# A fused attention and mixer kernel: from a scheduler's order to an order fixed by hand

## The chip, the cores and the metric

The kernel runs on one core of one Trainium2 chip. A core has five engines, each with its own instruction queue: TensorE (PE, matrix products; its weight loads are listed as PEld), VectorE (DVE), ScalarE (ACT), GpSimd (POOL) and SyncE (SP, which here only issues transfers). Each engine executes its queue in order and waits at an instruction whose inputs or buffers are not ready. [...]

The metric is the device time of the program in microseconds (us), as the median of several runs. Lower is better.

## The reference

For a batch of 8 with 8 heads, 576 positions and 64 values per head, the reference computes a windowed attention and then one token-and-channel mixer block:

```
rel = pos[:, None] - pos[None, :]
mask_plain = (rel >= 0) & (rel < 32)                       # heads 0..3
mask_dil   = (rel >= 0) & (rel < 128) & (rel % 4 == 0)     # heads 4..7
attn = softmax(where(mask, q @ k.T / 8, -1e9))
x    = (attn @ v), heads joined to 512 channels            # (8, 576, 512)
h    = relu(x.T @ w_tok1) @ w_tok2                         # over positions, 576 -> 256 -> 576
u    = x + h.T
out  = u + relu(u @ w_ch1) @ w_ch2                         # over channels, 512 -> 1536 -> 512
```

Inputs and output are float32; the kernel works in float16 with float32 sums in PSUM.

## The kernel before, in words

The work of one batch has two parts.

The *fill* computes attention and the token mixing. For each of four pairs of heads (hp 0 and 1 plain, 2 and 3 dilated) it transposes q and k on PE (`transposes`, L241; PSUM tiles `tp_q`, `tp_k`) and copies the results to SBUF: k by DVE into `kt`, the first head of q by DVE and the second by ACT into `qz`. The scores of a pair (`scores_plain` L268, `scores_dil` L302; PSUM tiles `sc` and, for the ends of the sequence, `sm`) are exponentiated by ACT into `attp` or `attd`, and multiplied by 0/1 masks (`band`, `dtail`), by DVE for batch 0 and by POOL for all others; the small tail part of a pair has an exponential and a mask of its own. For the dilated pairs, q is kept in four residue classes of positions, r, each 144 wide, so the queries after position 512 are read from it with a stride. The values of a head (`values` L328, PSUM tile `av`) are nine or six small matmuls, a reciprocal and a product on DVE into `xn`. Then follow the token mixing's first layer (`emit_h1` L361, PSUM `h1p`, relu on ACT into `h1`), its second with the residual (`emit_u` L373, PSUM `up`, five adds on DVE into `u16` and `u16t`), and the transpose of u (`emit_uT` L395, PSUM `tpu`, four copies on DVE and ACT in turn into `uT`).

The *main* part computes the channel mixing (`gen_main`, L469): 24 groups of four matmuls of 128 x 288 (`gp`, L480) with a relu by ACT or DVE in turn into `gt`, and eight groups of 12 matmuls of 128 x 256 (`yp`, L491 and L496), with an add on DVE (`o32`, L499) and two output transfers on SP after each second one. Odd batches have one more group of 12 x 512 columns for the last 64 rows of two batches (L506).

PSUM is shared out by tags: three banks `main` (gp, yp), three `sc`, two `fl` (tp, av, h1p, up, tpu).

While the main part of batch b runs, the fill of batch b+1 runs too, and q, k and v of batch b+2 are loaded by SP (`emit_loads`) and cast to float16 (`gen_casts`: q and the tails on ACT, k and v on POOL). The kernel writes these as streams of steps with assumed costs, and `drive` (L516) takes the stream that is least far along:

```
best = min(live, key=lambda st: st[1] / st[2] + st[3])
```

The framework's scheduler then reorders the instructions on each engine by its own estimate. So the final order on an engine is not the order of the source.

Before the loop stands the head: batch 0's loads on SP (one at a time, tails first), the weights w1, w2, w3 and w4 on POOL's queue, the fill of batch 0 without a main part beside it, and the loads and casts of batch 1. The weights are held back by small copies (`gate`, L544) that write one element of the target once some other data has come.

Of the kernel before, what the change touches and what calls it, by code (L numbers as in the profile page):

```python
# [9 lines left out]
FP16 = mybir.dt.float16  # L10
# [4 lines left out]
B = 8  # L15
# [53 lines left out]
def kernel(  # L69
# [39 lines left out]
    ident = fixed("ident", [128, 128])  # L109
    perm = [fixed(f"perm{i}", [128, 128]) for i in range(2)]  # L110
    band = fixed("band", [128, 1, 1, BLK])
    dtail = fixed("dtail", [128, 1, 2, 64])
    nc.sync.dma_start(out=ident, in_=nc.inline_tensor(np.eye(128, dtype=np.float16), name="ident128").ap())
    for i in range(2):
        nc.sync.dma_start(out=perm[i], in_=nc.inline_tensor(_np_perm(i), name=f"perm{i}").ap())
# [11 lines left out]
    w2 = [fixed(f"w2_{i}", [128, 640]) for i in range(2)]  # L127
    w2p = [fixed(f"w2p_{i}", [128, 4, 128]) for i in range(2)]
    w3 = [fixed(f"w3_{i}", [128, DCH]) for i in range(4)]
    w4 = [fixed(f"w4_{i}", [128, DM]) for i in range(NMB)]  # L130

    def emit_fixed():
        for hp in range(4):
            nc.gpsimd.memset(qz[hp][64:128, 0], 0.0)
            nc.gpsimd.memset(qz[hp][0:64, 1], 0.0)
            nc.gpsimd.memset(kt[hp][:, S:640], 0.0)
        for i in range(2):
            a = attp[i]
            nc.gpsimd.memset(
                a[:, :, 0:PTL].rearrange("p h (b c) -> p h b c", c=PST)[:, :, :, BLK:PST], 0.0)  # L140
            nc.gpsimd.memset(a[:, :, PTL:PW], 1.0)
            nc.gpsimd.memset(attd[i][:, :, DTL:DW], 1.0)
        for i in range(2):
            nc.gpsimd.memset(vv[i][64:128, 4], 0.0)
            nc.gpsimd.memset(vv[i][:, :, :, 64:65], 1.0)
            nc.gpsimd.memset(vt[i][:, :, 64:65], 1.0)
            nc.gpsimd.memset(w2[i][:, S:640], 0.0)
            nc.gpsimd.memset(w1t[i], 0.0)

# [3 lines left out]
    def load_qk(b, nm):  # L153
        t = sb.tile([128, H, 4, D], FP32, tag=f"l_{nm}", bufs=1, name=f"l_{nm}_{b}")
        l32[(b, nm)] = t
        for hp in range(4):
            nc.sync.dma_start(
                out=t[:, 2 * hp:2 * hp + 2].rearrange("m h r d -> m h (r d)"),
                in_=SRC[nm][b, 2 * hp:2 * hp + 2, 0:512, :].rearrange("h (m r) d -> m h (r d)", r=4))

    def load_tails_qk(b):
        t = sb.tile([128, H, D], FP32, tag="lt", bufs=1, name=f"lt_{b}")
        l32[(b, "t")] = t
        nc.sync.dma_start(out=t[0:64], in_=q[b, :, 512:S, :].rearrange("h s d -> s h d"))
        nc.sync.dma_start(out=t[64:128], in_=k[b, :, 512:S, :].rearrange("h s d -> s h d"))
# [18 lines left out]
    def emit_loads(b):  # L184
        load_tails_qk(b)
        load_qk(b, "q")
        load_qk(b, "k")
        load_v(b)
# [27 lines left out]
    def gen_casts(b):  # L216
        cast_tails_qk(b, nc.scalar)
        yield 1
        for hp in range(4):
            cast_qk(b, "q", hp, nc.scalar)  # L220
            yield 1
            cast_qk(b, "k", hp, nc.gpsimd)
            yield 1
        for i in range(2):
            cast_vn(b, 2 * i, nc.gpsimd)
            yield 1
            cast_vn(b, 2 * i + 1, nc.gpsimd)
            yield 1
            cast_vd(b, 2 * i, nc.gpsimd)
            yield 1  # L230
        cast_tail_v(b, nc.gpsimd)
        cast_vx(b, nc.gpsimd)
        yield 1
# [7 lines left out]
    def transposes(b, nm, hp):  # L241
        c = c16[(b, nm)]
        p = bank("fl", 2, f"tp_{nm}_{b}_{hp}", FP16)
        grid = p[:, 0:4 * RS].rearrange("p (r i) -> p r i", i=RS)
        for r in range(4):
            nc.tensor.transpose(  # L246
                out=grid[:, r, 0:128],
                in_=c[:, r, 2 * hp:2 * hp + 2, :].rearrange("m h d -> m (h d)"), identity=ident)
        nc.tensor.transpose(  # L249
            out=grid[:, :, 128:RS],  # L250
            in_=c16[(b, "t")][:, 2 * hp:2 * hp + 2, :].rearrange("m h d -> m (h d)"),
            identity=perm[nm == "k"])
        got = grid[:, :, 0:MR].rearrange("p r m -> p m r")
        if nm == "k":
            copy(nc.vector, natural(kt[hp][:, 0:S]), got)
        else:
            for h, eng in ((0, nc.vector), (1, nc.scalar)):
                rows = slice(64 * h, 64 * h + 64)
                o = qz[hp][rows, h]
                if hp < 2:  # L260
                    copy(eng, natural(o), got[rows])
                else:
                    copy(eng, o.rearrange("p (r m) -> p r m", r=4), grid[rows, :, 0:MR])
# [4 lines left out]
    def scores_plain(b, hp):  # L268
# [30 lines left out]
        mult(eng, tl, tl, band[:, 0, :, 0:64])  # L299
        yield 0.21  # L300

    def scores_dil(b, hp):  # L302
# [3 lines left out]
        for h in range(2):  # L306
            p = bank("sc", 3, f"sc_{b}_{hp}_{h}")
            for r in range(4):
                nc.tensor.matmul(  # L309
                    out=p[:, 128 * r:128 * r + 128], lhsT=kt[hp][:, r:512:4],  # L310
                    rhs=qz[hp][:, h, MR * r:MR * r + 128], start=True, stop=True)
# [3 lines left out]
        for h in range(2):  # L315
            qt = qz[hp][:, h].rearrange("p (r m) -> p m r", r=4)[:, 128:MR]
            for x, keys in enumerate((kt[hp][:, 384:512], kt[hp][:, 512:640])):
                nc.tensor.matmul(out=p[:, 128 * h + 64 * x:128 * h + 64 * x + 64], lhsT=keys,
                                 rhs=qt, start=True, stop=True)
# [5 lines left out]
        mult(eng, tl, tl, dtail)  # L325
# [35 lines left out]
    def emit_h1(b, jb):  # L361
        x = xn[b]
        j = slice(128 * jb, 128 * jb + 128)
        p = bank("fl", 2, f"h1p_{b}_{jb}")
        for c, w in ((slice(0, 256), w1n), (slice(256, 512), w1p)):
            nc.tensor.matmul(out=p[:, c], lhsT=w1t[b % 2][:, j], rhs=x[:, 4, c], start=True, stop=False)
            for s in range(4):
                nc.tensor.matmul(out=p[:, c], lhsT=w[:, s, j], rhs=x[:, s, c], start=False, stop=(s == 3))  # L368
        t = sb.tile([128, DM], FP16, tag="h1", bufs=4, name=f"h1_{b}_{jb}")
        relu(nc.scalar, t, p)  # L370
        return t
# [23 lines left out]
    def emit_uT(b, cb):  # L395
# [5 lines left out]
        eng = nc.scalar if cb % 2 else nc.vector  # L401
# [16 lines left out]
    GAP = 1.2  # L418

    def gen_fill(b):  # L420
        xn[b] = sb.tile([128, 5, DM], FP16, tag="xn", bufs=2, name=f"xn_{b}")
        if b % 2 == 0:
            u16t[b // 2] = sb.tile([128, DM], FP16, tag="u16t", bufs=2, name=f"u16t_{b // 2}")
            nc.vector.memset(u16t[b // 2][64:128], 0.0)

        def tp(hp):
            for nm in ("q", "k"):
                transposes(b, nm, hp)
                yield 0.25

        def sc(hp):
            yield from (scores_plain if hp < 2 else scores_dil)(b, hp)

        def va(hp):
            for h in (2 * hp, 2 * hp + 1):
                values(b, h)
                yield 0.29 if hp < 2 else 0.18

        yield from tp(0)
        yield from tp(1)  # L440
        yield from sc(0)
        yield from tp(2)
        yield from sc(1)
        yield from va(0)
        yield from tp(3)
        yield from sc(2)
        yield from va(1)
        yield from sc(3)
        yield GAP
        yield from va(2)  # L450
        yield GAP
        yield from va(3)
        yield GAP
        h1 = []
        for jb in range(2):
            h1.append(emit_h1(b, jb))
            yield 1.1
        yield GAP
        for s in (4, 0, 1, 2, 3):
            emit_u(b, s, h1)  # L460
            yield 0.44
        yield GAP
        for cb in range(4):
            emit_uT(b, cb)
            yield 0.25

    FILL = 2.0 + 1.22 + 1.13 + 1.88 + 2.2 + 2.2 + 1.0 + 5 * GAP

    def gen_main(b):  # L469
# [16 lines left out]
        for s in range(5 if odd else 4):  # L486
            p = bank("main", 3, f"yp_{b}_{s}")
            o32 = sb.tile([128, DM], FP32, tag="o32", bufs=3, name=f"o32_{b}_{s}")
            if s < 4:
                for mb in range(NMB):  # L490
                    nc.tensor.matmul(  # L491
                        out=p[:, 0:256], lhsT=gt[(b // 2, mb)][:, m0 + 128 * s:m0 + 128 * s + 128],
                        rhs=w4[mb][:, 0:256], start=(mb == 0), stop=(mb == NMB - 1))
                yield 1.31
                for mb in range(NMB):
                    nc.tensor.matmul(  # L496
                        out=p[:, 256:512], lhsT=gt[(b // 2, mb)][:, m0 + s:m0 + 512:4],
                        rhs=w4[mb][:, 256:512], start=(mb == 0), stop=(mb == NMB - 1))
                nc.vector.tensor_tensor(out=o32, in0=p, in1=u16[(b, s)], op=ALU.add)  # L499
                nc.sync.dma_start(out=out[b, 128 * s:128 * s + 128, 0:256], in_=o32[:, 0:256])  # L500
                nc.sync.dma_start(
                    out=out[b, 0:512, 256:512].rearrange("(m r) c -> r m c", r=4)[s], in_=o32[:, 256:512])
                yield 1.31
            else:
                for mb in range(NMB):
                    nc.tensor.matmul(out=p, lhsT=gt[(b // 2, mb)][:, 512:640], rhs=w4[mb],  # L506
                                     start=(mb == 0), stop=(mb == NMB - 1))
                nc.vector.tensor_tensor(out=o32, in0=p, in1=u16t[b // 2], op=ALU.add)
                nc.sync.dma_start(out=out[b - 1, 512:S, :], in_=o32[0:64])
                nc.sync.dma_start(out=out[b, 512:S, :], in_=o32[64:128])  # L510
                yield 2.6

    def main_cost(b):
# [105 lines left out]
```

## Time and profile before

| | us |
|---|---|
| median of 3 runs | 361.34 (360.73 to 362.38) |
| the profiled execution | 363.2 |
| its span, first to last instruction | 361.4 |
| PE busy | 309.3 (86%) |
| DVE busy | 186.3 (52%) |
| ACT busy | 146.2 (40%) |
| POOL busy | 146.3 (40%) |
| mean granted PE clock | 0.969 |
| DMA, all queues | 43.52 MB, mean 120 GB/s |

The page counts an engine as busy while an instruction of it executes. PE's matmuls overlap each other: the duration of one (288 ns for `gp`) is more than its share of the time (four in 0.49 us). A list of waits names the waiting engine, the line and the operation it stood at, and after the arrow the engine and line that released it, with the total in us, the number of waits and the longest. A timeline row gives the start, the length, the engine, the line, the operation and its tiles. A group row gives busy time and mean duration, and after the bar the idle time just before it with its releaser. The lines are those of the kernel before.

### The profile page before, as it was taken

What the parts mean: (1) busy time and instruction counts of PE and PEld (TensorE: products, weight loads), DVE (VectorE), ACT (ScalarE), POOL (GpSimd) and SP (SyncE); (2) the same over time, 40 slices, a digit from 0 to 9 for tenths busy, and PEclk for the clock granted to TensorE, in tenths of its full rate; (3) what the DMA queues carried; (4) which work ended last, traced back from release to release, by engine and by line L of the source; (5) the groups of instructions that cost most, each with busy time, mean ns of one, the idle gap of its engine ahead of it and who ended that gap; (6) DMA issues with size and microseconds to landing.
All of it is one profiled execution on the core that took longest, in us unless ns stands there. A gap on an engine that the chain in (4) does not pass through costs nothing.

```text
span 361.4 us, 7958 instructions
## 1 busy us (share of the span) xinstructions
PE 309.3 (86%) x3200; PEld 261.9 (72%) x3200; DVE 186.3 (52%) x401; ACT 146.2 (40%) x316; POOL 146.3 (40%) x201
## 2 busy tenths in 40 slices
PE   0626897499989997899899997899899998999994
PEld 0625576288877976688787976689788976888792
DVE  1727465226654456536664556536664456645421
ACT  2644277220683027721683027721682037412400
POOL 8774166932197006920296006920292006600000
PEclk9965899989999999999999999999999999999998
DMA  5999989856619520592019420532000120002012
GB/s 155 258 218 250 240 207 306 250 129 189 162 44 279 146 76 15 149 261 85 33 62 260 150 83 6 158 106 89 32 0 2 65 83 0 3 31 86 3 60 87
DMA packets 69588, 43.52 MB, mean 120 GB/s; under 512 B 37296, under 2 KB 68400, under 8 KB 69552
## 3 DMA queue, kind: packets, MB, share of 16 engines
q1 hardware_dynamic: 66128, 38.98, 38.2%
q0 software_dynamic: 3424, 4.03, 6.5%
q8 instruction: 25, 0.41, 0.5%
q14 instruction: 11, 0.09, 0.1%
HBM read 37.59 MB, written 9.44 MB: 130 GB/s over the span
## 4 chain that ended last, share of the span: by engine, by line
PE 53%; POOL 6%; ACT 5%; DVE 2%; issue 1%; DMA 1%; ACTq 0%; POOLq 0%
PE gp L480 13%; PE yp L496 10%; PE yp L491 10%; POOL attp L106 4%; PE h1p L368 3%; PE yp L506 3%; POOL attd L106 2%; ACT qz L94 2%; PE up L377 2%; PE up L380 1%; PE sc L309 1%; PE tp_q L246 1%; DVE qz L96 1%; PE tpu L413 1%; ACT attp L279 1%
## 5 line engine op out<-in xcount | busy, mean ns | idle before, releaser
L480 PE MATMUL gp<-uT,w 128*128 128x288 f16 x768 | 114.5, 288 | 1.9 <-ACT gt L100 1.9
L106 POOL TENSOR_TENSOR attp<-attp,band 128x1280 f16<-128x1280 f16 (+1 forms) x28 | 41.6, 1516 | 127.1 <-ACT attp L292 127.0
L480 PEld LDWEIGHTS <-w 128*128 128x128 f16 x768 | 71.1, 99 | 17.3 <-issue 2.6
L100 ACT ACTIVATE gt<-gp 128x288 f16<-128x288 f32 x96 | 39.7, 421 | 57.9 <-PE gp L480 57.6
L102 DVE TENSOR_SCALAR gt<-gp 128x288 f16<-128x288 f32 x96 | 43.2, 453 | 35.6 <-PE gp L480 32.1
L499 DVE TENSOR_TENSOR o<-yp,u 128x512 f32<-128x512 f32 x32 | 22.1, 692 | 56.2 <-PE yp L496 53.2
L491 PE MATMUL yp<-w,gt 128*128 128x256 f16 x384 | 48.5, 273 | 0.0
L496 PE MATMUL yp<-w,gt 128*128 128x256 f16 x384 | 47.2, 273 | 0.0
L496 PEld LDWEIGHTS <-gt 128*128 128x128 f16 x384 | 41.9, 114 | 0.3
L94 ACT COPY uT<-tpu 128x576 f16<-128x576 f16 x16 | 10.2, 639 | 74.6 <-PE tpu L407 69.8
L491 PEld LDWEIGHTS <-gt 128*128 128x128 f16 x384 | 37.3, 98 | 4.3
L106 DVE TENSOR_TENSOR xn<-av,rec 128x320 f16<-128x320 f32 x64 | 30.3, 487 | 1.3
L106 POOL TENSOR_TENSOR attd<-attd,band 128x1024 f16<-128x1024 f16 x14 | 29.8, 2129 | 1.7 <-ACT attd L312 1.6
L339 PE MATMUL av<-vv,attp 128*128 128x65 f16 x128 | 12.5, 200 | 18.8 <-POOL attp L106 12.1
L358 DVE RECIPROCAL rec<-av 128x5 f32<-128x5 f32 x64 | 11.2, 185 | 31.4 <-PE av L345 20.4
L246 PE MATMUL tp_q<-ident,c_q 128*128 128x128 f16 x128 | 13.4, 229 | 13.3 <-ACT c_q L94 9.3
L96 DVE COPY kt<-tp_k 128x576 f16<-128x576 f16 x32 | 23.9, 746 | 1.7 <-PE tp_k L249 1.6
L94 ACT COPY qz<-tp_q 64x576 f16<-64x576 f16 x32 | 20.3, 634 | 8.8 <-DVE qz L96 8.2
L383 DVE TENSOR_TENSOR u<-up,xn 128x512 f16<-128x512 f32 x32 | 21.2, 685 | 2.9 <-PE up L380 2.2
L246 PEld LDWEIGHTS <-c_q 128*128 128x128 f16 x128 | 9.9, 101 | 17.5 <-ACT c_q L94 10.9
L94 ACT CAST c_q<-l_q 128x512 f16<-128x512 f32 x32 | 19.6, 632 | 7.3 <-DMA l_q<-in_q_dram 3.6
L312 ACT ACTIVATE attd<-sc 128x512 f16<-128x512 f32 x32 | 18.7, 607 | 8.7 <-PE sc L309 8.5
(99 smaller groups left out, 515.2 us busy)
## 6 DMA issues: line engine op xcount, KB each, us to landing
out_dram<-o SPq DMA_DIRECT2D x72, 128.0 KB, 2.0
l_q<-in_q_dram SPq DMA_DIRECT2D x32, 256.0 KB, 4.5
l_k<-in_k_dram SPq DMA_DIRECT2D x32, 256.0 KB, 5.5
l_vn<-in_v_dram SPq DMA_DIRECT2D x32, 128.0 KB, 5.4
l_vd<-in_v_dram SPq DMA_DIRECT2D x16, 256.0 KB, 4.3
w<-in_moe_w_ch_dram POOLq DMA_DIRECT2D x12, 128.0 KB, 8.1
w<-in_moe_w_ch_dram POOLq DMA_DIRECT2D x4, 384.0 KB, 11.1
lt<-in_q_dram SPq DMA_DIRECT2D x8, 128.0 KB, 3.3
```

Source lines behind the costliest of these rows:

```text
L94: nc.scalar.copy(out=out, in_=in_)
L96: eng.tensor_copy(out=out, in_=in_)
L100: nc.scalar.activation(out=out, in_=in_, func=AF.Relu)
L102: eng.tensor_scalar_max(out=out, in0=in_, scalar1=0.0)
L106: eng.tensor_tensor(out=out, in0=x, in1=y, op=ALU.mult)
L246: nc.tensor.transpose(out=grid[:, r, 0:128], in_=c[:, r, 2 * hp:2 * hp + 2, :].rearrange("m h d -> m (h d)"), identity=ident)
L312: nc.scalar.activation(out=a[:, h, 0:DTL], in_=p, func=AF.Exp, scale=0.125)
L383: nc.vector.tensor_tensor(out=t, in0=p, in1=xn[b][:, s], op=ALU.add)
L480: nc.tensor.matmul(out=p[:, 0:288], lhsT=w3[cb][:, 128 * mb:128 * mb + 128], rhs=uT[(b, cb)][:, 288 * sh:288 * sh + 288], start=(cb == 0), ...
L491: nc.tensor.matmul(out=p[:, 0:256], lhsT=gt[(b // 2, mb)][:, m0 + 128 * s:m0 + 128 * s + 128], rhs=w4[mb][:, 0:256], start=(mb == 0), stop ...
L496: nc.tensor.matmul(out=p[:, 256:512], lhsT=gt[(b // 2, mb)][:, m0 + s:m0 + 512:4], rhs=w4[mb][:, 256:512], start=(mb == 0), stop=(mb == NM ...
L499: nc.vector.tensor_tensor(out=o32, in0=p, in1=u16[(b, s)], op=ALU.add)
```

## The change

`drive`, `gen_fill` and `gen_casts` go. The kernel calls `tc.manual_schedule()`, so each engine executes in source order, and the source fixes that order:

```diff
+    def fill_steps(b):
...
+        for hp, at in ((0, 0.2), (1, 1.6), (2, 4.6), (3, 8.0)):
+            for i, nm in enumerate(("q", "k")):
+                steps.append((at + 0.7 * i, 0.28, lambda nm=nm, hp=hp: transposes(b, nm, hp)))
+        for hp, at in ((0, 3.0), (1, 6.4), (2, 9.8), (3, 12.6)):
+            scores(hp, at)
+        for hp, at in ((0, 12.0), (1, 14.6), (2, 18.4), (3, 21.4)):
+            for h in range(2):
+                steps.append((at + 0.7 * h, 0.29 if hp < 2 else 0.18,
+                              lambda h=h, hp=hp: values(b, 2 * hp + h)))
+        for half, at in ((0, 19.4), (1, 24.0)):
+            for jb in range(2):
+                steps.append((at + 0.7 * jb, 0.55, lambda jb=jb, half=half: emit_h1(b, jb, half, h1[jb])))
+        for i, s in enumerate((4, 0, 1, 2, 3)):
+            steps.append((26.4 + 0.9 * i, 0.44, lambda s=s: emit_u(b, s, h1)))
         for cb in range(4):
+            steps.append((31.4 + 0.6 * cb, 0.28, lambda cb=cb: emit_uT(b, cb)))
+        return steps
...
+    def interleave(main, steps):
+        steps = sorted(steps, key=lambda st: st[0])
+        t = 0.0
+        while main is not None or steps:
+            if steps and (main is None or steps[0][0] <= t):
+                _, cost, fn = steps.pop(0)
+                fn()
+                t += cost
+            else:
+                try:
+                    t += next(main)
+                except StopIteration:
+                    main = None
...
     for b in range(B):
+        steps = []
+        if b + 2 < B:
+            emit_loads_qk(b + 2)
+            load_v(b + 2)
+            steps += [(19.0 + 0.9 * i, 0.0, f) for i, f in enumerate(cast_steps(b + 2))]
         if b + 1 < B:
+            steps += fill_steps(b + 1)
+        interleave(gen_main(b), steps)
```

`t` is an emission clock in assumed us; it decides only the order.

Work also changes engine. All casts of a later batch run on POOL (`cast_steps`: tails, q and k in turn, v, 17 in all). `kt` is copied by ACT, and so are the second halves of `uT` (cb 2 and 3; cb 0 and 1 on DVE). The tail masks go to DVE for every batch, and the memsets of `qz` and `kt` too. For hp 2 and 3, q is transposed flat, with its classes 128 wide and the positions from 512 on in one run of 64, so that the tail scores read it without a stride:

```diff
+        flat = nm == "q" and hp >= 2
         for r in range(4):
             nc.tensor.transpose(
+                out=p[:, 128 * r:128 * r + 128] if flat else grid[:, r, 0:128],
...
+        if flat:
+            nc.tensor.transpose(out=p[:, 512:640], in_=tail, identity=ident)
+            nc.vector.tensor_copy(out=qz[hp][0:64, 0], in_=p[0:64, 0:S])
+            nc.scalar.copy(out=qz[hp][64:128, 1], in_=p[64:128, 0:S])
+            return
...
         if nm == "k":
-            copy(nc.vector, natural(kt[hp][:, 0:S]), got)
+            nc.scalar.copy(out=natural(kt[hp][:, 0:S]), in_=got)
...
-        mult(eng, tl, tl, dtail)
+        mult(nc.vector, tl, tl, dtail)
...
-                                 rhs=qt, start=True, stop=True)
+                                 rhs=qz[hp][:, h, 512:S], start=True, stop=True)
```

`emit_h1` works by halves of 256 channels (plain heads, dilated heads), each with its own bank and relu. In the main part, `yp` groups are cut in two of six matmuls between which other steps can stand; odd batches compute the tail rows first; and in the last batch the last tile is added and written in two halves:

```diff
+        for s in ((4, 0, 1, 2, 3) if odd else (0, 1, 2, 3)):
...
+                        if mb == 5:
+                            yield 0.65
+                    if last and s == 3:
+                        nc.vector.tensor_tensor(out=o32[:, c], in0=p[:, c], in1=u16[(b, s)][:, c], op=ALU.add)
```

The head is written out. The identity, the permutations and the masks are one constant loaded at once. The first loads of q go by SP's queue and those of k by ACT's; a one-element exponential (`spark`) stands early on ACT; the weights go by POOL's queue behind a gate on the last q, with w3 ahead of w4 (three transfers now); batch 1's q and k wait by a gate for the last of w3; and 29 matmuls on a tile of zeros (`warm`, 128 x 512 each) stand between the steps of batch 0:

```diff
+    load_qk(0, "q", 0, 2, nc.sync)
+    load_qk(0, "k", 0, 2, nc.scalar)
+    nc.scalar.dma_start(out=const, in_=const_dram)
+    load_tail(0, "q", nc.sync)
+    load_tail(0, "k", nc.scalar)
...
+    gate(w1n[0:1, 0, 0:1], l32[(0, "q")][0:1, 7, 0, 0:1])
...
+    warm(10)
...
+    start_casts(0)
+    cast_tails_qk(0, nc.vector)
+    tp[0]()
+    tp[1]()
+    start_casts(1)
+    for hp in range(4):
+        for f in sc[3 * hp:3 * hp + 3]:
+            f()
+        if hp < 3:
+            tp[2 * hp + 2]()
+            tp[2 * hp + 3]()
+        if hp < 2:
+            start_casts(hp + 2)
+        warm(3)
...
+    for nm in ("q", "k"):
+        gate(l32[(1, nm)][0:1, 0, 0, 0:1], w3[3][0:1, 0:1])
+        load_qk(1, nm, 0, 4, nc.sync)
+        load_tail(1, nm, nc.sync)
+        load_qk(1, nm, 4, 8, nc.sync)
+    load_v(1)
+    for f in cast_steps(1):
+        f()
```

## The prediction, before the result was known

> **What bounds it now.** I read the engines' shares and slices first, then who waited for whom on TensorE, then the timeline, to cut the span at the first `gp` matmul of each batch's main part.
>
> ```profile
> PE 309.3 (86%) x3200; PEld 261.9 (72%) x3200; DVE 186.3 (52%) x401; ACT 146.2 (40%) x316; POOL 146.3 (40%) x201
> ...
> PEclk9965899989999999999999999999999999999998
> DMA  5999989856619520592019420532000120002012
> ```
>
> PE is the bound with holes in it; in the first eighth its clock is halved while the DMA engines are full. The waits of PE (us in total, times, longest):
>
> ```profile
> PE av L339 <- POOL attp L106: 12.1, 7, 2.2
> PE tp_q L246 <- ACT c_q L94: 9.3, 1, 9.3
> PE av L350 <- POOL attd L106: 6.8, 4, 3.0
> PE av L339 <- POOL vv L96: 6.0, 2, 5.0
> ```
>
> The values (`av`) stand so close behind their scores that PE, which keeps its order, waits for POOL's masks. The timeline at the start of each main part (start, length, work):
>
> ```profile
> 45.30 0.29 PE L480 MATMUL gp<-uT,w 128*128 128x288 f16 x1
> 91.93 0.65 PE L480 MATMUL gp<-uT,w 128*128 128x288 f16 x4
> 132.74 0.65 PE L480 MATMUL gp<-uT,w 128*128 128x288 f16 x4
> 172.79 0.65 PE L480 MATMUL gp<-uT,w 128*128 128x288 f16 x4
> 213.66 0.65 PE L480 MATMUL gp<-uT,w 128*128 128x288 f16 x4
> 253.71 0.65 PE L480 MATMUL gp<-uT,w 128*128 128x288 f16 x4
> 294.15 0.65 PE L480 MATMUL gp<-uT,w 128*128 128x288 f16 x4
> 331.68 1.51 PE L480 MATMUL gp<-uT,w 128*128 128x288 f16 x11
> ```
>
> So: head 45.3; iterations 0 to 6 of 46.6, 40.8, 40.1, 40.9, 40.1, 40.4, 37.5 (286.4); then a bare main part and tail, 29.7. Gap-free spacing by the timeline gives the floor of an iteration: 24 `gp` groups of 0.49, 8 `yp` of 1.31, 8 transposes of 0.275, scores 2 x 0.61 and 2 x 0.88, values 4 x 0.29 and 4 x 0.18, `h1` 4 x 0.545, `up` 5 x 0.435, `tpu` 4 x 0.275: 35.1, and 37.7 in odd batches (2.6 for their tail rows). Loss now: 5 and 3, in iteration 0 11.5.
>
> Prices of the moved copies and masks (busy, mean ns of one):
>
> ```profile
> L106 POOL TENSOR_TENSOR attp<-attp,band 128x1280 f16<-128x1280 f16 x14 | 36.5, 2606 | 127.1 <-ACT attp L292 127.0
> L96 DVE COPY kt<-tp_k 128x576 f16<-128x576 f16 x32 | 23.9, 746 | 1.7 <-PE tp_k L249 1.6
> L94 ACT COPY qz<-tp_q 64x576 f16<-64x576 f16 x32 | 20.3, 634 | 8.8 <-DVE qz L96 8.2
> L318 PE MATMUL sm<-qz,kt 128*128 128x64 f16 x64 | 9.7, 285 | 0.0
> ...
> ```
>
> **Steady iterations, part by part.** *Values 9 us behind their scores:* the emission clock puts the plain scores at 3.1 to 4.7 and their values at 12.4; in between POOL needs one mask of 2.6. All POOL waits of PE go (3.1 us of iteration 4: 1.67 + 1.08 + 0.33). POOL then holds four masks (9.5) and 17 casts (8.8) in 36 us, casts last; even a mask held up 3 us is hidden.
>
> *Stride-free q for heads 4 to 7:* the 8 small `sm` matmuls are spaced 0.108 now, the like-sized L289 ones 0.03: minus 0.62 per iteration. Floor 34.5 and 37.1.
>
> *kt copies DVE to ACT, casts of q and tails ACT to POOL, tail masks POOL to DVE:* ACT loses 5 casts (0.58 each back to back, 2.9) and gains 4 kt copies. ACT shows none of that shape; bounds are its uT copy of the same 128x576 (0.64) and DVE's 0.75. I take 0.66, the spacing of ACT's qz. The sum stays; the place doesn't: transposes, scores and copies now crowd the first 13.8 us of the clock. ACT's work there by back-to-back spacing: qz and kt 8 x 0.66, exponentials 2 x 1.42 and 2 x 1.26, 9.4 relus x 0.30: 13.4, so almost full, and its qz copy starts only after DVE's, as now:
>
> ```profile
> 173.76 0.75 DVE L96 COPY qz<-tp_q 64x576 f16<-64x576 f16 x1
> 174.60 0.63 ACT L94 COPY qz<-tp_q 64x576 f16<-64x576 f16 x1 [0.71 <-DVE qz L96]
> ```
>
> I walked the fixed order by hand with these spacings and PSUM buffers (2 `fl`, 3 `sc`, 3 `main`). PE stops (a) at the second pair of transposes, 0.9: their `fl` banks are held by qz, then kt, both on ACT; (b) at `gp` group 4.1, 1.1: its bank waits for an ACT relu, behind qz of pair 2, behind DVE's qz, behind DVE's tail mask (0.2), which waits for ACT's last exponential; (c) at `gp` 7.1, 0.4, and the first `yp`, 0.5, the same way. That is 2.9. Values, `up` and `tpu` fit: DVE's adds take 0.61 each at steps of 0.9. uT copies 2 and 3 both on ACT (2 x 0.64) end 0.2 after an even iteration's last `yp`. `h1` in halves costs ACT about 0.5 (four relus near 0.42 for two of 0.60) where it waited 27.5 us in total: nothing, 3.5 in all if that cover went. The loads for two batches on stand on SP ahead of this iteration's outputs and behind the last one's; they wait only for casts that ended some 8 us earlier, and fewer, larger q and k transfers (4 issues for 8) keep SP shorter: nothing. If they came 5 us late, the casts at 19 would, and the next transposes, 17 us on, still not. The `yp` cut in quarters moves only the places where other work slips in; tail rows first in odd batches cost nothing, since their inputs are an iteration old.
>
> Iterations: even 34.5 + 2.9 + 0.2 = 37.6, odd 37.1 + 2.9 = 40.0; 4 x 37.6 + 3 x 40.0 = 270.4, 16.0 less than 286.4. Iteration 0 gives 9 of it: the masks, which waited behind casts of late v, are in time (after k's tails, below, the last 0.5 MB of k, v's 1.2 and the rest of w4 take 10: v of batch 1 lands near 53, is cast by 54, and the first mask ends near 57; its values are due 14.7 after the start, near 59).
>
> **The head.** Two chains; the later one sets the start.
>
> *Batch 0:* the first q and k lead on two queues, so the first transposes start near 6.8, not 9.35. ACT's table load (1.28, it ran at 6.86 behind the tails) and the single load of constants lie beside that transfer. The memsets of qz and kt go from POOL (8 x 0.57 and 4 x 0.14, 5.1) to DVE; the trace has no such row for DVE, between 0 and 5.1, and DVE sat idle for 6.6 before its first cast: nothing, at most 0.9 if they run to 5.9. POOL's gate now holds all weight loads and v's casts behind it until q is complete; the weights were first issued at 11.8 before, so little moves. Then each head pair is a round trip on ACT (cast 0.58, qz 0.66, kt 0.66, exponentials 1.3) and DVE (mask about 1.1, qz 0.6), serial in the new order: 5.0. Four from 7.2 end at 27; eight values at DVE's 0.62, 32; `h1` and four warm-up matmuls 3, five `up` at 0.6, `tpu` and copies 2.5: 41.5 with a full clock. PE's clock stood at 0.50 from 22 to 38 although PE was busy 62% of it; if the 29 warm-up matmuls don't prevent that, `h1` doubles: 44.
>
> *Batch 1:* w3 now precedes w4, and batch 1's q and k wait for w3. With q and k of batch 0 in at 12.5 (their last cast began at 14.98; the lead of 2.5 comes off), the last w3 can be issued once w1n has landed (7.1 after its issue), near 20; its 11 to 13 us to landing give 32. Then 1.84 MB of q and k up to k's tails, with about half of w4's 1.57 MB beside it, at the 240 GB/s of 12 to 38 us: 11. Three POOL casts, 1.9: 44.9, less 0.5, since one `gp` group stands before the first transposes. I take 44.5 (bounds 41.5, batch 0 alone, and 49, all of w4 first): minus 0.8.
>
> [...]
>
> **The tail:** the last add is half as wide (0.69 to 0.35) and one output issue (0.5) no longer trails: minus 0.8.
>
> **Sum:** 16.0 + 0.8 + 0.8 = 17.6 off the profiled execution's 363.2 (span 361.4): 345.6. That execution is 1.9 above the median 361.3 of the three runs, so 343.7 there.
>
> **Rivals.** *Buffers absorb more (17%):* only the chain in (b) that no buffer hides stays, 1.2: 7 x 1.7 = 11.9 less, 331.8. For: ACT's average is 40%. Against: its 13.4 of 13.8.
>
> *Late loads (13%):* start at 49 or 50, 349. For: full DMA engines until 54; against: nothing else is asked of them.
>
> *ACT sets the pace, slower (10%):* if ACT's waits are not overlapped, four qz handoffs of 0.85 and four mask handoffs of 0.5 add 5.4 to its 13.4 in each iteration: 18.8 against 13.8, loss 5.0 + 0.6 instead of 2.9, so 7 x 2.7 = 18.9 more, 362.6. It decides from a loss of 5.4. Against: before, ACT waited for DVE's qz 8.2 us in all, not the 24 of this case.
>
> *No effect (5%):* what POOL's waits give, ACT's in-order waits take to within 2 us. Against: PE's POOL waits alone are 20 us.
>
> **How the numbers follow.** Forecast 55%: loss per iteration 2 to 4, start 42 to 47, 335 to 353. With the rivals' 331.8, 349 and part of 362.6 the range is 330 to 358. About 0.5% is what a measurement of this kernel can tell from no change. Faster 0.85 (55 + 17 + 13), same 0.05, slower 0.10.
>
> **What would show it.** Right: no PE wait for POOL after iteration 0; the first `gp` near 44.5; main parts 37 to 40 apart; ACT near full in the first 14 us of each, PE's remaining holes released by ACT; `sm` of L318 near 200 ns. Wrong: iterations over 42 with PE released by ACT or DVE throughout, a start past 50, or PE dense there (loss under 1.5).

## The result, and the profile after

The changed kernel takes 385.7 us (383.6 to 386.7) beside 361.9 us for the kernel before on the same chip: 1.065 times as long (95% interval 1.058 to 1.071). The prediction of 343.7, with a range of 330 to 358, was wrong in sign.

Lines below are those of the changed kernel; L106 is still the helper that multiplies, L460 the `gp` matmul, L257 and L258 the copies of the flat q by DVE and ACT. The engines' shares and slices of the changed kernel:

```profile
PE 324.9 (85%) x3229; PEld 263.1 (69%) x3229; DVE 215.8 (56%) x403; ACT 145.3 (38%) x328; POOL 144.0 (38%) x190
...
PEclk9587998999989998999989998999989998999999
DMA  8999996025902177013921159011940210001012
```

DVE has two more instructions than before and 29.5 us more busy time. PE is busy 15.6 us longer: the 29 warm-up matmuls take 11.5, the `gp` matmuls 10.6 more than before (125.1 for 114.5) at a clock that now dips in every iteration (granted 0.96 over each of the seven; before, 0.96 over the first and 1.00 over the others), and the stride-free `sm` matmuls 4.8 less. The waits of the changed kernel (engine and line that waited, releaser, us in total, times, longest):

```profile
ACT qz L258 <- DVE qz L257: 44.9, 16, 3.9
...
PE gp L460 <- DVE gt L102: 29.1, 18, 3.1
```

The waits for POOL at the values are gone, as predicted. In their place PE waits for DVE's relu, and ACT for DVE's half of q. The timeline at the start of three main parts:

```profile
43.86 0.81 PE L460 MATMUL gp<-uT,w 128*128 128x288 f16 x3
87.97 0.78 PE L460 MATMUL gp<-uT,w 128*128 128x288 f16 x4
134.06 0.65 PE L460 MATMUL gp<-uT,w 128*128 128x288 f16 x4
```

With the others (176.83, 222.86, 265.63, 311.63, 354.40) the iterations are 44.1, 46.1, 42.8, 46.0, 42.8, 46.0, 42.8. The prediction's sum can be set against the profiled execution's 385.6, part by part: start 43.9 (44.5 was predicted), seven iterations 310.5 (270.4), last main part and tail 29.4 (28.9), 1.8 around the span. The whole miss of 40.0 lies in the steady iterations. The groups of the changed kernel that differ (busy us, mean ns of one, after the bar the idle time before them):

```profile
L106 DVE TENSOR_TENSOR attp<-attp,const 128x128 f16<-128x128 f16 x16 | 37.9, 2369 | 19.6 <-ACT attp L297 19.6
L106 POOL TENSOR_TENSOR attp<-attp,const 128x1280 f16<-128x1280 f16 x14 | 36.5, 2607 | 140.9 <-ACT attp L294 140.9
...
L106 DVE TENSOR_TENSOR attd<-attd,const 128x256 f16<-128x256 f16 x16 | 16.8, 1048 | 17.9 <-ACT attd L321 17.9
```

The tail masks that moved to DVE take 2.37 and 1.05 us on average. On POOL they took 0.43 and 0.67, and on DVE in batch 0 of the changed kernel the small one takes 0.22. One of them in the timeline (start, length, and in brackets the idle time before it):

```profile
94.92 2.60 POOL L106 TENSOR_TENSOR attp<-attp,const 128x1280 f16<-128x1280 f16 x1 [17.79 <-ACT attp L294]
94.98 2.62 DVE L106 TENSOR_TENSOR attp<-attp,const 128x128 f16<-128x128 f16 x1 [0.90 <-ACT attp L297]
...
97.52 0.44 DVE L257 COPY qz<-tp_q 64x576 f16<-64x576 f16 x1
97.89 0.44 DVE L102 TENSOR_SCALAR gt<-gp 128x288 f16<-128x288 f32 x1
98.05 0.63 ACT L258 COPY qz<-tp_q 64x576 f16<-64x576 f16 x1 [3.11 <-DVE qz L257]
98.38 0.65 PE L460 MATMUL gp<-uT,w 128*128 128x288 f16 x4 [2.37 <-DVE gt L102]
```

POOL's large mask and DVE's tail mask of the same pair are released by neighbouring exponentials, start 0.06 apart and end 0.08 apart. The DVE instruction is a tenth of the other's size. Behind it in DVE's queue stand the copy of q and a relu, behind these ACT's copy and a `gp` bank, and PE stops for 2.37. The copy and the relu themselves, which read PSUM (`tp_q` and `gp`), take their usual 0.44. In the chain that ended last, DVE holds 27% and these two masks alone 14%.

So the theory (A): a DVE mask that works in SBUF (where `attp` and `attd` lie) is held for as long as POOL's mask beside it runs. The rivals: (B) ACT's full in-order queue is the pace and the slow masks lie in its shadow; (C) the masks are slow on DVE for a reason of their own; (D) DVE simply has too much work; (E) the two masks of a pair write the same tile, and it is the tile that ties them together.

### The profile page after: what moved, and what is told of

The parts are those of the page before. It is cut to its first block, busy times and chain, and to the rows that moved or that the text cites. A ratio compares the mean times of both kernels' runs of the same rounds, so it can differ in the third digit from the quotient of the medians.

```text
span 383.8 us, 7936 instructions
## 1 busy us (share of the span) xinstructions
PE 324.9 (85%) x3229; PEld 263.1 (69%) x3229; DVE 215.8 (56%) x403; ACT 145.3 (38%) x328; POOL 144.0 (38%) x190
## 4 chain that ended last, share of the span: by engine, by line
PE 43%; DVE 27%; ACT 15%; DMA 10%; issue 2%; SPq 1%; POOL 1%; ACTq 0%; POOLq 0%
PE yp L475 22%; DVE attp L106 10%; PE gp L460 5%; DVE xn L106 5%; DMA l_vt<-in_v_dram 4%; DVE attd L106 4%; DVE gt L102 3%; ACT attp L281 3%; PE yp L495 3%; DVE qz L264 3%; DMA lt<-in_k_dram 3%; ACT gt L100 2%; PE h1p L370 2%; ACT kt L262 2%; ACT qz L265 2%
## 5 line engine op out<-in xcount | busy, mean ns | idle before, releaser
L460 PE MATMUL gp<-uT,w 128*128 128x288 f16 x768 | 125.1, 300 | 31.9 <-DVE gt L102 29.1
L460 PEld LDWEIGHTS <-w 128*128 128x128 f16 x768 | 74.1, 102 | 51.5 <-issue 35.6
L106 POOL TENSOR_TENSOR attp<-attp,const 128x1280 f16<-128x1280 f16 x14 | 36.5, 2607 | 140.9 <-ACT attp L294 140.9
L100 ACT ACTIVATE gt<-gp 128x288 f16<-128x288 f32 x96 | 40.7, 424 | 37.8 <-PE gp L460 36.9
L102 DVE TENSOR_SCALAR gt<-gp 128x288 f16<-128x288 f32 x96 | 42.3, 448 | 20.8 <-PE gp L460 20.7
L106 DVE TENSOR_TENSOR attp<-attp,const 128x128 f16<-128x128 f16 (+1 forms) x18 | 39.6, 2207 | 25.6 <-ACT attp L297 19.6
L106 POOL TENSOR_TENSOR attd<-attd,const 128x1024 f16<-128x1024 f16 x14 | 29.8, 2137 | 24.7 <-ACT attd L314 24.7
L100 ACT ACTIVATE h<-h1p 128x256 f16<-128x256 f32 x32 | 12.3, 383 | 63.2 <-PE h1p L370 63.2
L106 DVE TENSOR_TENSOR xn<-av,rec 128x320 f16<-128x320 f32 x64 | 31.5, 491 | 2.2
L106 DVE TENSOR_TENSOR attd<-attd,const 128x256 f16<-128x256 f16 (+1 forms) x18 | 18.3, 1025 | 23.1 <-ACT attd L321 17.9
L258 ACT COPY qz<-tp_q 64x576 f16<-64x576 f16 x16 | 10.1, 633 | 44.9 <-DVE qz L257 44.9
L262 ACT COPY kt<-tp_k 128x576 f16<-128x576 f16 x32 | 20.4, 637 | 0.6
L281 ACT ACTIVATE attp<-sc 128x480 f16<-128x480 f32 x32 | 17.6, 588 | 0.3 <-PE sc L278 0.3
L264 DVE COPY qz<-tp_q 64x576 f16<-64x576 f16 x16 | 12.0, 749 | 9.4 <-PE tp_q L260 9.1
L96 POOL CAST c_k<-l_k 128x512 f16<-128x512 f32 x28 | 17.1, 612 | 0.0
```

Of the source, the lines that this page charges most:

```text
L96: eng.tensor_copy(out=out, in_=in_)
L100: nc.scalar.activation(out=out, in_=in_, func=AF.Relu)
L102: eng.tensor_scalar_max(out=out, in0=in_, scalar1=0.0)
L106: eng.tensor_tensor(out=out, in0=x, in1=y, op=ALU.mult)
L262: nc.scalar.copy(out=natural(kt[hp][:, 0:S]), in_=got)
L264: nc.vector.tensor_copy(out=natural(qz[hp][0:64, 0]), in_=got[0:64])
```

## The experiments

**The tail masks back on POOL.**

```diff
-        mult(nc.vector, tl, tl, band[:, 0, :, 0:64])
+        mult(eng, tl, tl, band[:, 0, :, 0:64])
...
-        mult(nc.vector, tl, tl, dtail)
+        mult(eng, tl, tl, dtail)
```

> Edit: in the changed kernel the tail masks of batches 1 to 7 go back from DVE to POOL; nothing else. Theory A (a DVE mask with two SBUF inputs is held for as long as POOL's mask beside it runs, and everything behind it on DVE is late): the held time goes, 2 x (2.67 - 0.43) + 2 x (1.11 - 0.67) is about 5.4 of DVE's queue per iteration, 7 x 5.4 = 38 less than 385.7, so 343 to 350; the waits of ACT's qz copy for DVE fall from 44.9 us to under 12, those of gp for DVE's relus from 29.1 to under 5, iterations to 38 to 40.5. Rival B (ACT's full in-order queue, with the kt copies on it, is the pace, and the slow masks lie in its shadow): 372 to 386, iterations still 42.8 and 46.

Measured: 335.7 us, 0.926 of the kernel before (0.921 to 0.931). Two changed lines are worth 50 us. Iterations are 35.7 and 38.4 from the second on (36.4 the first). No wait of PE for DVE's `gp` relu is left among its waits. The list of PE's waits begins now with those of the head:

```profile
PE sc L311 <- ACT kt L262: 4.6, 2, 3.0
PE sc L278 <- ACT kt L262: 3.3, 2, 1.6
PE tp_q L260 <- DVE c_t L96: 2.2, 1, 2.2
```

Rival B falls. The time is even below theory A's 343 to 350: that sum took 5.4 of held time per iteration off, and the iterations became 7.1 and 7.6 shorter (shares below).

**The tail masks on DVE, but ahead of the large ones.** In each pair the tail exponential and mask come before what releases POOL's mask:

```diff
-            out=blocks[:, :, 3, 0:BLK], in_=p[:, 0:320].rearrange("p (h c) -> p h c", c=BLK),
-            func=AF.Exp, scale=0.125)
-        nc.scalar.activation(
             out=tl, in_=p[:, 320:448].rearrange("p (h c) -> p h c", c=64), func=AF.Exp, scale=0.125)
+        mult(nc.vector, tl, tl, band[:, 0, :, 0:64])
+        nc.scalar.activation(
+            out=blocks[:, :, 3, 0:BLK], in_=p[:, 0:320].rearrange("p (h c) -> p h c", c=BLK),
+            func=AF.Exp, scale=0.125)
```

(and the same way for the dilated pairs, where the tail's part moves between the two heads).

> Edit: the tail masks stay on DVE, but in each pair's step the tail exponential and the tail mask stand ahead of the work that releases POOL's large mask, so that the two masks of a pair do not run at the same time. Theory A: the DVE masks of 128x128 return to about 0.22 us and those of 128x256 to 0.56 to 0.6, although they are still on DVE, and the time is 343 to 352. Rival C (the masks are slow on DVE in steady state for a reason of their own, such as the tile or the engine's other work, and not for what POOL does at that moment): they stay at 1 to 2.6 us and the time at 378 to 388.

Measured: 338.2 us, 0.937 (0.931 to 0.943). The groups of this kernel:

```profile
L106 DVE TENSOR_TENSOR attd<-attd,const 128x256 f16<-128x256 f16 x16 | 9.6, 603 | 10.0 <-ACT attd L323 10.0
...
L106 DVE TENSOR_TENSOR attp<-attp,const 128x128 f16<-128x128 f16 x16 | 4.0, 252 | 15.4 <-ACT attp L294 15.4
```

The same instructions on the same engine take a ninth and three fifths of the time when POOL is not in a mask; the plain ones now run in 0.23. Of the dilated ones every second still starts inside a POOL mask: 0.29 alone, 1.01 beside it. C falls, and the cause is the moment, not the engine.

**All masks on DVE.** `mask_engine` returns DVE for every batch.

> Edit: all masks of all batches on DVE, as batch 0 has them; POOL has only its casts. Theory A: DVE takes on about 2 x 1.1 + 2 x 0.8 = 3.8 us per iteration of large masks but loses the 6.0 of held time, so it is faster than the changed kernel: 350 to 368. Rival D (DVE is late because of how much it is given, whatever POOL does): more work on DVE, slower, over 390.

Measured: 360.4 us, 0.996 (0.994 to 0.998), iterations of 39.8 and 42.4. DVE does more work and the kernel is 25 us faster than the changed one: D falls. DVE's extra work is still paid: PE waits 16.1 us for its relus, where the run with the tails on POOL has none. The hold also goes the other way here, in a stretch where POOL casts (timeline of this kernel):

```profile
97.21 0.61 POOL L96 CAST c_t<-lt 128x512 f16<-128x512 f32 x1 [29.73 <-PE tp_k L260]
97.37 1.68 DVE L106 TENSOR_TENSOR attp<-attp,const 128x1280 f16<-128x1280 f16 x2 [1.73 <-ACT attp L294]
97.77 1.21 POOL L96 CAST c_q<-l_q 128x512 f16<-128x512 f32 x1
98.92 0.62 POOL L96 CAST c_k<-l_k 128x512 f16<-128x512 f32 x1
```

The two DVE masks take 0.96 where POOL is idle and 1.68 here, having waited for the cast already running; the next cast takes 1.21 instead of 0.62. The casts and the masks share no tile, so E falls as well.

**POOL's masks cut in two.**

```diff
-        mult(eng, blocks[:, :, :, 0:BLK], blocks[:, :, :, 0:BLK], band)
+        for h in range(2):
+            mult(eng, blocks[:, h:h + 1, :, 0:BLK], blocks[:, h:h + 1, :, 0:BLK], band)
...
-        mult(eng, diag, diag, band[:, :, :, 0:128])
+        for h in range(2):
+            mult(eng, diag[:, h:h + 1], diag[:, h:h + 1], band[:, :, :, 0:128])
```

> Edit: the changed kernel with each large mask on POOL cut in two instructions, one per head; the tail masks stay on DVE. If a DVE mask is held only until the POOL instruction that runs at that moment ends, the 128x128 one is held about 1.3 instead of 2.6 us and the 128x256 one ends near the first half's end, about 0.7: the extra DVE time per iteration falls from 6.0 to about 3.2, and of the 50 us between the changed kernel and the one with the tails on POOL about 27 remain: 355 to 370. If it is held until POOL's queue has no mask left, the means stay at 2.4 and 1.05 and the time at 380 to 390.

Measured: 359.1 us, 0.992 (0.989 to 0.995). The DVE masks now take 1.39 and 0.33 on average. Two rows of the groups of this kernel:

```profile
L106 POOL TENSOR_TENSOR attp<-attp,const 128x640 f16<-128x640 f16 x28 | 38.5, 1400 | 126.1 <-PE tp_k L260 107.4 <-ACT attp L294 18.7
...
L106 DVE TENSOR_TENSOR attp<-attp,const 128x128 f16<-128x128 f16 x16 | 22.3, 1394 | 19.6 <-ACT attp L297 19.6
```

The held time follows the length of one POOL instruction, 1.40, and not that of POOL's queue: DVE gets in between two of them. One of the 14 did not. In iteration 0, DVE's mask started beside a cast and ended only with the second half of POOL's mask:

```profile
52.68 0.67 POOL L96 CAST vv<-l_vt 64x512 f16<-64x512 f32 x1
...
53.03 3.53 DVE L106 TENSOR_TENSOR attp<-attp,const 128x128 f16<-128x128 f16 x1 [0.90 <-ACT attp L297]
53.23 0.47 POOL L96 CAST vt<-l_vx 128x256 f16<-128x256 f32 x1
...
53.67 2.80 POOL L106 TENSOR_TENSOR attp<-attp,const 128x640 f16<-128x640 f16 x2
```

The changed kernel has the like there, 3.40. So a hold can outlast the instruction that it began beside; what decides it no run here shows.

**One SBUF input instead of two.** In the changed kernel the plain heads' tail mask is replaced:

```diff
-        mult(nc.vector, tl, tl, band[:, 0, :, 0:64])
+        nc.vector.tensor_scalar_max(out=tl, in0=tl, scalar1=0.0)
```

> Edit: the changed kernel with the plain heads' tail mask (two SBUF inputs) replaced by a maximum with zero on the same 128x128 tile on DVE (one SBUF input, float16), which leaves that mask out; the dilated heads' tail masks stay as a control. If two SBUF inputs are what is held, the plain one takes about 0.2 us beside POOL's mask and the time falls by about two thirds of the 50 us, to 347 to 356; if any DVE instruction that reads and writes SBUF alone is held, it stays at 2.4 us and the time at 380 to 390.

Measured: 384.3 us, 1.062 (1.059 to 1.066), and the instruction is held just the same: 2.59, where it takes 0.18 in batch 0 (timeline of this kernel):

```profile
95.25 2.60 POOL L106 TENSOR_TENSOR attp<-attp,const 128x1280 f16<-128x1280 f16 x1 [17.75 <-ACT attp L294]
95.31 2.59 DVE L301 TENSOR_SCALAR attp<-attp 128x128 f16<-128x128 f16 x1 [0.90 <-ACT attp L297]
```

My expectation that two inputs are what matters was too narrow. This float16 operation from SBUF to SBUF with one input is held too. Those that read PSUM are not: in the run with the tails on POOL, 55 of DVE's 96 `gp` relus start inside a POOL mask and take 0.456 on average, the others 0.455, and `xn` takes 0.492 either way.

Why the two engines hold each other no trace here shows.

**The same move in the kernel before.** Its tail masks of batches 1 to 7 go to DVE, nothing else.

> Edit: the kernel before, with its tail masks of batches 1 to 7 moved from POOL to DVE and nothing else. Theory A: the hold does not depend on the fixed order; the DVE masks take 1 to 2.6 us here too and PE, which waits for DVE's relus and copies, loses 1 to 5 per iteration: 365 to 395. Rival: the scheduler's order, with DVE idle for 48%, hides it: 358 to 363.

Measured: 368.9 us, 1.018 (1.014 to 1.022): 7 us slower. The masks are held there too, 1.70 and 1.13 us on average. So the hold does not come from the fixed order. Its cost differs much, 7 us here and 50 there, although DVE is held almost as long: 5.2 us per iteration against 6.6. A part of this is that here the move also pays. It frees POOL, and PE's waits for POOL's masks at the values fall from 20.7 us (12.1, 6.8 and 1.8) to 10.7:

```profile
PE av L339 <- POOL attp L106: 6.5, 4, 1.6
...
PE av L350 <- POOL attd L106: 4.2, 3, 2.2
```

In the fixed order there were no such waits to win back, and the copy of q and a relu stand right behind each plain pair's mask. How much of the rest the scheduler's order hides I have not traced.

**The kt copies back on DVE,** on top of the tails on POOL.

```diff
-            nc.scalar.copy(out=natural(kt[hp][:, 0:S]), in_=got)
+            nc.vector.tensor_copy(out=natural(kt[hp][:, 0:S]), in_=got)
```

> Edit: the tail masks on POOL as in the first of these runs and the four kt copies of an iteration back on DVE. It prices the loss of 2.9 per iteration that the prediction put down to ACT's crowded first 14 us. If that was right, ACT loses 4 x 0.64 = 2.6 there and the time falls by 7 to 14 against the first of these runs; if PE's remaining gaps have other causes, the two are within 3 us.

Measured: 331.4 us, 0.915 (0.912 to 0.918), 4.3 less than the run with the kt copies on ACT, between the two expectations. Iterations are 35.1 and 37.8 to the tenth, 0.6 less than 35.7 and 38.4. PE's listed waits from 82 to 300 us come to 2.6 us in all. The kt copies on ACT cost 0.6 per iteration, about a fifth of the 2.9 that I had given to ACT's crowding.

**The values near their scores,** on top of that.

```diff
-        for hp, at in ((0, 12.0), (1, 14.6), (2, 18.4), (3, 21.4)):
+        for hp, at in ((0, 5.4), (1, 8.8), (2, 12.2), (3, 15.0)):
```

> Edit: tail masks on POOL, kt copies on DVE, and the values of a pair only 2.4 instead of 9 us of the emission clock behind their scores (12.0, 14.6, 18.4, 21.4 become 5.4, 8.8, 12.2, 15.0). Theory: the distance is what hides POOL's masks, so PE's waits for POOL at the values come back, 2 to 3 us for each of four pairs less what overlaps, 3 to 9 per iteration: 350 to 395. Rival: the order alone is enough and the distance gives nothing: 329 to 335.

Measured: 397.8 us, 1.100 (1.097 to 1.104), 66 more than without this edit, 9.5 per iteration. PE's waits in this kernel:

```profile
PE av L340 <- POOL attp L106: 29.3, 14, 4.1
PE av L351 <- POOL attd L106: 15.9, 13, 1.4
PE av L354 <- POOL attd L106: 4.3, 13, 0.3
```

The distance is what makes this fixed order good. The listed waits are 49.5 of the 66, 7.1 per iteration, where the kernel before waited 3.1 for POOL in iteration 4. PE's clock over the iterations also fell, from 1.00 to 0.96, which I estimate at 13 (0.04 x 322).

**The head without its warm-up matmuls** (all `warm` calls left out, on top of the kt copies on DVE).

> Edit: tail masks on POOL, kt copies on DVE, and the 29 warm-up matmuls of the head left out. By the prediction's head the first batch's chain took 41.5 with a full clock and 44 with a halved one, and the second batch's loads 44.5 set the start: without them the clock reads 0.5 from 20 us on and the start moves by at most 1.5 us either way. Rival: the first batch's chain ends last, and then the halved clock costs 2 to 5 us (333.5 to 336.5).

Measured: 330.5 us, 0.913 (0.910 to 0.916), no difference from 331.4 that the intervals support. The first `gp` came at 41.5 instead of 46.2, but iteration 0 took 40.1 instead of 35.8: what starts earlier waits for batch 1's loads (PE stands 3.0 at 42.9 for POOL's cast of its q). The forecast for the clock was wrong: it did not fall to 0.5 without them. The clock slices, first with the 29 matmuls, then without:

```profile
PEclk9585699999999999999999999999999999999999
```

```profile
PEclk9999989999999999999999999999999999999999
```

**w4 behind batch 1's q and k** (on top of the last). The three w4 transfers leave their place behind w3 and come behind POOL's first five casts of batch 1:

```diff
-    for f in cast_steps(1):
+    early = cast_steps(1)
+    for f in early[:5]:
+        f()
+    for i in range(3):
+        nc.gpsimd.dma_start(
+            out=w4a[:, 4 * i:4 * i + 4],
+            in_=moe_w_ch2[512 * i:512 * i + 512, :].rearrange("(i p) c -> p i c", p=128))
+    for f in early[5:]:
         f()
```

> Edit: tail masks on POOL, kt copies on DVE, no warm-up matmuls, and the three w4 transfers issued on POOL behind its first five casts of batch 1 instead of behind w3. If batch 1's loads set the end of iteration 0 (without the warm-up matmuls the start came 4.7 earlier and iteration 0 took 4.3 more), its q and k land up to 6.5 earlier (1.57 MB at about 240 GB/s) and the time falls by 1.5 to 4 against 330.5, to 326.5 to 329. Rival: w4 then comes late for the first yp, or v's tails of batch 0 set the start: 330 to 335.

Measured: 328.3 us, 0.906 (0.903 to 0.909), 2.2 less than without it, as expected; the two ran on different chips, but the intervals of their ratios do not overlap. POOL's first cast of batch 1 starts at 39.45 instead of 44.60. The first main part starts later, at 43.3 instead of 41.5, but the second at 79.1 instead of 81.6. This is the fastest kernel of the study, 33.6 below the kernel before.

**All first loads on SP's queue,** once on the kernel with the kt copies on DVE and once on the one with the late w4:

```diff
-    load_qk(0, "k", 0, 2, nc.scalar)
-    nc.scalar.dma_start(out=const, in_=const_dram)
+    load_qk(0, "k", 0, 2, nc.sync)
+    nc.sync.dma_start(out=const, in_=const_dram)
```

(and the other loads of k the same way).

> Edit: tail masks on POOL, kt copies on DVE, and all first loads (q, k, constants, tails) on SP's queue instead of half of them on ACT's. By the prediction the second queue gives 2.5 us at the front and nothing by the start of the main part, since loads set it: within 1.5 of 331.4, the first transposes 1 to 2.5 later. Rival: the head is one chain from the first load to the first gp group, and all of the front is lost: 332.5 to 334.

> Edit: the kernel of the late w4 with all first loads on SP's queue. Theory: the first transposes start within 0.3 of those with two queues (5.45 and 5.55 in the runs so far) and the time is within 1.0 of that kernel's. Rival: the second queue is worth the 2 us that the medians of the earlier pair (333.4 against 331.4, on different chips) show: 1.5 to 2.5 above it.

Measured: 333.4 (0.920, 0.917 to 0.924) and 331.1 us (0.914, 0.912 to 0.917). The first pair is 2.0 apart (both are on record with chip 11, not with different chips) and decides nothing: the intervals overlap a little, and the traces, one queue's fastest execution and two queues' slowest, have the first `gp` 2.1 earlier with one queue. The second pair ran on one chip and is 2.8 apart. The theory missed there, in the time and in the first transposes, which start 0.6 apart and not within 0.3 (5.79 against 5.20). The rival's time came, but not its place: the last scores of batch 0 start 1.5 earlier with one queue. What comes later is v. PE's first waits at the values, first with two queues and then with one:

```profile
PE av L346 <- ACT vv L94: 3.0, 1, 3.0
```

```profile
PE av L346 <- ACT vv L94: 6.3, 1, 6.3
```

v's tail rows are the last load on SP before batch 1; with k in the same queue they are issued at 13.82 instead of 12.62, and the matmul that needs them starts 1.8 later. That leaves 1.6 at the first `gp` (44.88 against 43.29) and, with 0.3 from a later iteration, the 2.0 between the two profiled executions; the rest of the 2.8 lies in executions that no trace shows.

## Why the prediction was wrong, point by point

- **The step that failed: "DVE's tail mask (0.2)" in chain (b).** It was priced by DVE's rows of batch 0, where POOL runs no mask, and the condition was not named. Beside POOL's mask the term measured 2.62 for a plain pair and 1.80, 0.28 or 0.8 to 0.9 for a dilated one. Against 0.22 in batch 0 and 0.29 in the run with the tails first, that is 2 x 2.4 for the plain pairs and about 1.5 + 0.3 for the dilated ones, 6.6 of DVE's queue per iteration. The iterations are 7.1 and 7.6 longer than with the masks on POOL. PE's waits for DVE's relus are 4.2 of it (29.1 / 7), its waits for ACT's relus and at the tail rows, which the run with the masks on POOL does not have, 0.5 (2.3 and 1.4 in all). The clock, granted 0.96 over these iterations and 1.00 over those of that run, I estimate at 1.8 (0.04 x 44.4). The rest, about 0.9, I have not traced. A sign stood in the profile of the kernel before: its DVE ran the 128x256 tail mask twice in batch 0, once beside a cast on POOL and once without, and took 0.83 and 0.28.

```profile
26.83 0.68 POOL L96 CAST vv<-l_vd 128x512 f16<-128x512 f32 x1
26.90 0.83 DVE L106 TENSOR_TENSOR attd<-attd,dtail 128x256 f16<-128x256 f16 x1
...
34.05 0.28 DVE L106 TENSOR_TENSOR attd<-attd,dtail 128x256 f16<-128x256 f16 x1
```

- **The in-order chain was right but for its last link.** The prediction walked ACT's qz behind DVE's qz behind DVE's tail mask; that is in the trace. But it had PE's `gp` bank wait for an ACT relu behind them, and PE waited for DVE's own relu behind DVE's qz: 29.1 us, against 2.3 for ACT's. The rival for "slower" (ACT sets the pace) named the neighbouring engine and a loss of 5.6; the loss was 8.3 and 8.9 against the floors 34.5 and 37.1.
- **The floor was added up wrongly.** Its terms, as listed, come to 34.8 and not 35.1. So the floors would be 34.1 and 36.7, the forecast 2.4 lower, and every loss over the floor named here 0.3 to 0.4 larger. It changes neither the sign nor the cause.
- **Values 9 us behind: right.** PE's steady waits for POOL vanished, and bringing the values near costs 9.5 per iteration in this order.
- **The loss of 2.9 from ACT's crowding: too large.** Without the holds the iterations are 35.7 and 38.4, 1.2 and 1.3 over the floor; with kt on DVE 0.6 and 0.7. The size is near that of the rival "buffers absorb more", whose 331.8 stands near the 335.7 and 331.4 measured, but not its place: it kept (b), and with the masks on POOL PE's waits show only (a), 0.3 for qz and 0.2 for kt in an iteration (2.1 and 1.6 us in seven waits each). Without the held mask, (b) and (c) don't appear.
- **Stride-free q: right.** The `sm` matmuls read 203 ns against 285, and kt on ACT 0.64, as bounded.
- **The head: the start was right (43.9 for 44.5), but partly by luck.** Batch 1's chain came near the 44.9 that was walked: its first transposes start at 45.05, without a wait. But the first `gp` at 43.86 was released by batch 0's chain, which ended at about the same time, with the clock at 0.54 from 10 to 20 us in spite of the warm-up matmuls. Two parts were wrong. v's tail, which PE waited 2.1 for, was on neither chain of the working; the second queue was credited with the front; it is worth 2.8, of which the trace shows 2.0, 1.6 of it by the first `gp` through v. The forecast that the clock would be halved without warm-up matmuls fell: it was granted 1.00 from 0 to 40 us.
- **The tail:** 29.4 for 28.9; near enough.

Without the one mis-sized term the forecast would have had the right sign: the same kernel with that move undone takes 335.7, and with the move kept but most of the hold avoided 338.2, both within the range of 330 to 358.

## What to carry to other kernels

A duration read from a row holds only for what ran beside it (0.22 us for the plain tail mask in batch 0, 2.62 beside POOL's); when work moves to another engine, look for a row in which that engine and its neighbour run at once, and ask what the moved instruction will start next to. Between DVE and POOL, keep operations from SBUF to SBUF apart in time (0.25 us on average for that mask ahead of POOL's, 2.37 in the changed kernel), or cut POOL's into shorter instructions (1.39), or leave both on one engine (the kernel took 335.7 us with both on POOL and 360.4 with both on DVE, instead of 385.7). In an order fixed by hand, a held instruction is paid by everything behind it (here PE stopped for 2.37 behind a hold of 2.62), so put the distance between producer and consumer, and nothing urgent behind an instruction that can be held.

## What the runs showed of the hardware

- Two stalls of PE of 2.37 and 2.21 us, 4 us apart, were followed by a granted clock of 0.64 from 104 to 106 us and 0.50 from 106 to 108 in the changed kernel, in which PE was busy 1.17 and 2.00 of 2 us. Whether the stalls caused the drop no run here shows.
- The three kernels without warm-up matmuls were granted 0.994 to 1.000 over the span in all 15 executions; the four with them that take 331 to 339 us 0.962 to 0.985. In the head the matmuls of zeros were followed by drops (0.57 and 0.55 in the second and fourth ten us of the run with kt on DVE). The kernel before, which has none, ranges from 0.959 to 1.000, so their absence does not decide it alone, and the cause stays open.
